# Linear attention and a token layer on one core: the middle key tile projected in row tiles into the banks of h, with a new order

## The chip, the core and the metric

The kernel runs on one core of a Trainium2 chip. The metric is device time in microseconds (us): the median of three timed runs, 710.31 us before the change (709.31 to 710.52). Beside the timed runs one execution was profiled; all rows of a view come from it.

Engines: PE multiplies matrices (PEld is its loading of weights), DVE works on vectors, ACT evaluates functions and copies, POOL (GpSimd) is a second vector engine, SP issues the DMAs. Each runs its own instructions in program order and waits on semaphores for the others.

## The reference

Linear attention over 8 batches, 8 heads, 576 tokens and 64 dimensions with exponential features, then a layer over all 4608 tokens.

```python
def phi(x):
    proj = np.einsum('bhsd,df->bhsf', x, w_phi)
    proj = proj - np.max(np.abs(proj), axis=-1, keepdims=True)
    return np.concatenate([np.exp(proj), np.exp(-proj)], axis=-1)
q_p, k_p = (phi(q), phi(k))
kv = np.einsum('bhsf,bhsd->bhfd', k_p, v)
z = np.sum(k_p, axis=2)
num = np.einsum('bhsf,bhfd->bhsd', q_p, kv)
den = np.einsum('bhsf,bhf->bhs', q_p, z)[..., None] + 1e-06
x = (num / den).transpose(0, 2, 1, 3).reshape(B * S, H * D)

h = x @ w_in
e = np.exp(h - np.max(h, axis=-1, keepdims=True))
solu = h * (e / (np.sum(e, axis=-1, keepdims=True) + 1e-09))
mu, var = np.mean(solu, -1, keepdims=True), np.var(solu, -1, keepdims=True)
out = ((solu - mu) / np.sqrt(var + 1e-06) * g_ln) @ w_out
```

`w_phi` is 64 x 128, `w_in` 512 x 1024, `w_out` 1024 x 512.

## The kernel before

**Attention in 16 units.** A unit u is half a batch: two pairs of heads, each pair two heads of 64 dimensions that fill the 128 partitions. The 576 keys of each pair are four tiles of 128 tokens and a half tile of 64; the half tiles of the unit's two pairs lie together in one *middle key tile* of 128 tokens. So a unit has three key groups (`GROUPS`, line 32): four outer tiles of the first pair (g = 0), the middle tile (g = 1), four outer tiles of the second pair (g = 2).

Keys are projected on PE by `kp`. For the outer groups `k_rows` calls `by_rows` (line 527): for each tile one matmul a head, with the 64 rows of that head alone (128 tokens by 128 features, 64 x 128 of the array), the two heads into two different banks; 8 matmuls in all. For the middle tile `k_mid` calls `by_block` (line 536): one matmul over all 128 rows against `wph`, which holds `w_phi` twice, block-diagonally, with zeros elsewhere; it gives 256 columns in one bank. Behind the projection DVE takes `km` (maximum of absolute values, writes `m`) and `ks` (subtraction, writes `dk`), both reading the bank; ACT takes two exponentials of `dk` into `ek`. All are called `pjk`, `m`, `dk` and `ek` in the profile. [...]

Queries of units 0 to 2 (`Q_PLAIN`) go the same way (`pjq`, `dq`, transposed as `dT`); later ones are projected transposed (`pq`, four half blocks a pair of heads), turned by DVE (`blk`), and get their maximum over a small PE transposition (`mtp`), DVE `mt`, POOL `mb` and a second one (`mcp`). `visit` (line 599) then does on PE, in one piece, the numerators of the pair before (`num`), the products of keys and values (`kvT`) and the denominators (`den`).

**Tokens in 36 tiles of 128.** `moe_h` (line 1084) makes `h` in two halves of 12 matmuls (fp32r, from high and low parts of x and `w_in`); `moe_max` (DVE, `nm`), `moe_exp` (ACT, `eu`) and `moe_u` (DVE, `eu<-h,eu`) read its banks in turn, and the last of them frees them. The result is transposed by a DVE pass (`ub`) and DMAs (`du`, `uTs`), split into high and low parts (`uhs`, `uls`), and multiplied with `w_out` by `moe_o` (`o`, two halves of 12).

**PSUM.** Eight banks: `a` has three buffers of one bank, `kv` one, `h` one buffer of two banks, `mo` two of one (`PSUM_BUFS`, line 46). `h` serves the token tiles. In the units of `EARLY` (0, 1, 2) key and query groups use `h` and `mo`; from unit 3 on, all key groups, `pq`, `mtp`, `mcp`, `num` and `den` share `a`.

**What sets the order.** Each step is an entry of a plan (`op`, `add`) with an engine, what it comes after, and the buffers that it takes and uses. `SEQUENCE` (line 57) is a list of 2623 numbers: the entries in the order in which they are written out, which is the order on every engine and on SP's queue; `Plan.order` (line 240) asserts that nothing stands ahead of what it needs. A buffer goes to whoever comes next in that list. The costs in the entries play no part in the written order.

Of the kernel before, what the change touches and what calls it, by code (L numbers as in the profile page):

```python
# [18 lines left out]
DM, DF = 512, 1024  # L19
NTOK = B * S  # L20
P = 128
# [1303 lines left out]
```

## Time and profile before

| what | us |
|---|---|
| median of three timed runs | 710.31 |
| the profiled execution, whole | 708.93 |
| its span, first to last instruction | 707.1 |
| PE busy | 694.5 |
| POOL busy | 512.3 |
| DVE busy | 478.1 |
| ACT busy | 368.2 |

The busy time of the groups that the change touches, over the whole span: the 512 records of outer key tiles (`pjk`, 64*128) 39.4 us, the 32 records of middle tiles (`pjk`, 128*128) 10.8 us, and the three `h` groups of 288 records 93.7, 89.5 and 89.0 us. Records of PE overlap, so that their lengths add up to more than their share of time; what a piece costs is read from the starts of its neighbours. DVE's idle time ahead of `nm` is 64.5 us in sum, ended by PE's `h`.

### The profile page before, as it was taken

The page shows a single profiled execution, that of the slowest core. Times are in us where ns is not written, and L with a number is a line of the kernel's source. Part 1 is how long each engine was busy: PE and PEld are TensorE (multiplying, and loading weights), DVE is VectorE, ACT ScalarE, POOL GpSimd, SP SyncE. Part 2 cuts the span into 40 slices and gives each one's busy share as a digit, 9 for nine tenths or more (in the row PEclk, how much of TensorE's full clock was granted, in tenths as well). Part 3 has the DMA queues.
Part 4 walks back from the last instruction along what each step waited for, and adds up shares of the span by engine and source line. Part 5 has one row for each costly group of instructions (what it writes and reads, how often), then busy time and mean ns, then how long its engine had stood idle before and what let it go on. Part 6 is the DMA issues. An engine that isn't in the chain of part 4 may idle for free.

```text
span 707.1 us, 13443 instructions
## 1 busy us (share of the span) xinstructions
PE 694.5 (98%) x4894; PEld 520.2 (74%) x4894; DVE 478.1 (68%) x795; ACT 368.2 (52%) x684; POOL 512.3 (72%) x500
## 2 busy tenths in 40 slices
PE   8999999999999999999999999999999999999997
PEld 6666676777777777777777777777787777788886
DVE  6999787647867668577675777857567775354531
ACT  4997744626545564455554656535554554233231
POOL 1156999997878888789788997978868878361341
PEclk9999999999999999999999999999999999999999
DMA  8954465545575565566545555556374435320331
GB/s 293 339 191 120 114 199 163 157 115 161 162 214 151 143 201 151 166 167 193 144 116 162 188 164 156 173 164 191 107 201 156 127 109 149 94 94 24 124 116 67
DMA packets 113778, 110.04 MB, mean 156 GB/s; under 512 B 57648, under 2 KB 91184, under 8 KB 113200
## 3 DMA queue, kind: packets, MB, share of 16 engines
q1 hardware_dynamic: 113712, 109.18, 51.5%
q8 instruction: 39, 0.64, 0.4%
q14 instruction: 27, 0.22, 0.1%
HBM read 76.75 MB, written 32.39 MB: 154 GB/s over the span
## 4 chain that ended last, share of the span: by engine, by line
PE 64%; POOL 1%; DMA 1%; issue 1%; DVE 1%; ACT 0%; SPq 0%; ACTq 0%; POOLq 0%
PE h L271 22%; PE o L271 22%; PE kvT L271 6%; PE num L271 5%; PE pjk L271 3%; PE pq L271 3%; PE den L271 2%; DMA du<-ub 1%; DMA uTs<-du 0%; POOL xa L271 0%; PE uT L271 0%; PE mcp L271 0%; PE mtp L271 0%; POOL uls L271 0%; POOL zacc L271 0%
## 5 line engine op out<-in xcount | busy, mean ns | idle before, releaser
L271 ACT ACTIVATE ek<-dk 128x512 f32<-128x512 f32 (+1 forms) x160 | 87.2, 583 | 64.5 <-DVE dk L271 64.4
L271 PE MATMUL o<-w_out_h,uhs 128*128 128x512 f32 x264 | 105.3, 399 | 0.0
L271 PE MATMUL o<-w_out_h,uls 128*128 128x512 f32 x264 | 103.3, 391 | 0.1
L271 PE MATMUL o<-w_out_l,uhs 128*128 128x512 f32 x264 | 103.1, 390 | 0.0
L271 POOL TENSOR_TENSOR uls<-uTs,uhs 128x1024 fp32r<-128x1024 f32 x33 | 79.1, 2396 | 25.3 <-ACT uhs L271 22.9
L271 PE MATMUL h<-win_h,mxh 128*128 128x512 f32 x288 | 93.7, 406 | 0.0
L271 PE MATMUL h<-win_l,mxh 128*128 128x512 f32 x288 | 89.5, 392 | 0.0
L271 PE MATMUL h<-win_h,mxl 128*128 128x512 f32 x288 | 89.0, 390 | 0.0
L271 DVE TENSOR_REDUCE nm<-h 128x1 f32<-128x1024 f32 x36 | 43.7, 1215 | 64.5 <-PE h L271 64.4
L271 ACT ACTIVATE fq<-pT 128x576 f32<-128x576 f32 x104 | 68.4, 676 | 20.9 <-DVE pT L271 20.8
L271 POOL TENSOR_TENSOR zt<-ek 128x512 f32<-128x512 f32 x52 | 67.2, 1292 | 15.1 <-ACT ek L271 14.2
L271 POOL TENSOR_TENSOR hq<-rawq,hq 64x1152 fp32r<-64x1152 f32 x26 | 68.9, 2652 | 8.9 <-ACT hq L271 4.2
L271 PE MATMUL num<-fq,kvf 128*64 128x288 f32 x512 | 68.9, 412 | 0.8 <-DMA kvf<-dk 0.5
L271 ACT ACTIVATE eu<-h,nm 128x1024 f32<-128x1024 f32 x36 | 40.2, 1116 | 56.4 <-DVE nm L271 45.8
L271 DVE STREAM_TRANSPOSE blk<-pq 128x288 f32<-128x288 f32 x104 | 45.3, 459 | 28.2 <-PE pq L271 23.7
L271 DVE TENSOR_REDUCE m<-pjk 128x4 f32<-128x512 f32 (+1 forms) x80 | 48.5, 622 | 22.9 <-PE pjk L271 22.7
L271 PEld LDWEIGHTS h<-win_h,mxl 128*128 128x128 f32 x288 | 54.0, 188 | 12.1
L271 PEld LDWEIGHTS h<-win_l,mxh 128*128 128x128 f32 x288 | 54.0, 188 | 12.0
L271 PE MATMUL kvT<-ek,rawv 128*64 128x256 f32 x512 | 61.1, 380 | 0.0
L271 POOL TENSOR_TENSOR blk<-blk,mcol 128x1152 f32<-128x1152 f32 x26 | 55.4, 2131 | 5.7 <-PE h L271 3.5
L271 PEld LDWEIGHTS h<-win_h,mxh 128*128 128x128 f32 x288 | 50.7, 189 | 10.7 <-DVE kvs L271 0.5
L271 PEld LDWEIGHTS o<-w_out_h,uls 128*128 128x128 f32 x264 | 49.5, 188 | 11.5 <-POOL uls L271 0.7
(109 smaller groups left out, 1425.4 us busy)
## 6 DMA issues: line engine op xcount, KB each, us to landing
du<-ub SPq DMA_DIRECT2D x33, 512.0 KB, 2.9
uTs<-du SPq DMA_DIRECT2D x132, 128.0 KB, 3.1
rawq<-in_q SPq DMA_DIRECT2D x26, 576.0 KB, 4.6
rb<-d SPq DMA_DIRECT2D x64, 144.0 KB, 3.3
out<-os SPq DMA_DIRECT2D x35, 256.0 KB, 2.9
rawk<-in_k SPq DMA_DIRECT2D x32, 256.0 KB, 4.5
rawv<-in_v SPq DMA_DIRECT2D x32, 256.0 KB, 3.8
dk<-kvs SPq DMA_DIRECT2D x28, 192.0 KB, 1.9
```

Of the source, the lines that this page charges most:

```text
L271: return self.tc.keep_in_program_order(method(*args, **kwargs))
```

## The change

From unit 3 on the middle tile is projected by a new `k_mid_rows`: two matmuls, each head with its own 64 rows and its own 128 columns of `wph`, the first into the first bank of `h`, the second into the second. `tokens`, which gives DVE its view of a projection, reads such a tile as two pieces of 128 columns, 512 apart. The entry `kp` of the middle tile takes `h` in place of a buffer of `a`. Units 0 to 2 keep `by_block`.

```diff
+    def k_mid_rows(st):
+        pj = bank("h", [P, DF], "pjk")
+        for j, r in enumerate(HEADS):
+            nc.tensor.matmul(
+                pj[:, 512 * j : 512 * j + F], lhsT=st["rk", 1][r, :P], rhs=wph[r, j * F : (j + 1) * F],
+                start=True, stop=True,
+            )
+        st["pj", 1] = {None: pj}
...
     def tokens(pj, n):
+        if pj.shape[1] == DF:
+            return pj.rearrange("p (j c) -> p j c", j=2)[:, :, :F]
         return pj[:, : n * F].rearrange("p (t f) -> p t f", f=F)
...
             ktag = K_BANKS[g] if u in EARLY else "a"
-            add(("kp", g), "tensor", mm32(256) if g == 1 else 4 * 224, z, k_mid if g == 1 else k_rows,
-                (ktag,) if g == 1 else (g, ktag), [("kl", g), ("abs", "wp")],
-                banks(ktag, "pj", g), [("rk", g)])
+            if g == 1 and u not in EARLY:
+                ktag = "h"
+                add(("kp", g), "tensor", 224, z, k_mid_rows, (), [("kl", g), ("abs", "wp")], banks(ktag, "pj", g), [("rk", g)])
+            else:
...
 SEQUENCE = (
-    99, 3, 2, 88, 0, 132, 126, 7, 136, 102, 4, 100, 101, 90, 103, 104, 5, 127, 107, 95, 89, 91, 230, 130, 14,
...
```

`SEQUENCE` is new as a whole; all engines' instructions stand in another order. Three places of it follow.

**Unit 3, PE.** Before, from the end of token tile 0 (`h`, low part of x) to the start of token tile 2:

```order
L271 MATMUL h<-win_h,mxl 128x512 x2
L271 MATMUL dT<-ident,dq 128x128 x3
L271 MATMUL pjk<-wph,rawk 128x256
L271 MATMUL mtp<-ident,m_1218 36x128
L271 MATMUL dT<-ident,dq 128x128 x3
L271 MATMUL pjk<-wph,rawk 128x128 x8
L271 MATMUL pq<-hq,w_hh 128x288
L271 MATMUL pq<-hq,w_l_76 128x288
L271 MATMUL h<-win_h,mxh 128x512 x2
```

After, the same stretch:

```order
L271 MATMUL h<-win_h,mxl 128x512 x2
L271 MATMUL mtp<-ident,m_1256 36x128
L271 MATMUL dT<-ident,dq 128x128 x6
L271 MATMUL pjk<-wph,rawk 128x128 x10
L271 MATMUL mcp<-ident,mb_77 128x128
L271 MATMUL pq<-hq,w_hh 128x288
L271 MATMUL pq<-hq,w_l_76 128x288
L271 MATMUL h<-win_h,mxh 128x512 x2
```

The middle tile (128x256) stood between transpositions; its two matmuls now stand directly behind the 8 of the second outer group, as one row of 10, with the small transposition `mcp` behind them.

**Unit 3, DVE.** Before, the passes from the maximum of token tile 0 on:

```order
L271 TENSOR_REDUCE nm<-h 128x1
L271 TENSOR_REDUCE m<-pjk 128x2
L271 TENSOR_REDUCE mt<-mtp 36x32
L271 TENSOR_TENSOR dk<-pjk,m 128x256
L271 TENSOR_TENSOR eu<-h,eu 128x1024
L271 TENSOR_REDUCE m<-pjk 128x4 x2
```

After:

```order
L271 TENSOR_REDUCE nm<-h 128x1
L271 TENSOR_REDUCE mt<-mtp 36x32
L271 TENSOR_TENSOR eu<-h,eu 128x1024
L271 TENSOR_REDUCE m<-pjk 128x2
L271 TENSOR_TENSOR dk<-pjk,m 128x256
L271 TENSOR_REDUCE m<-pjk 128x4 x2
```

The two passes over the middle tile (`m` 128x2 and `dk` 128x256) stood ahead of the pass that frees `h` (`eu<-h,eu`) and now stand behind it.

**Unit 5, PE.** Before, from the end of token tile 4 on; the rows of `o` behind begin half an `o`, 12 matmuls:

```order
L271 MATMUL h<-win_h,mxl 128x512 x2
L271 MATMUL pjk<-wph,rawk 128x128 x8
L271 MATMUL pjk<-wph,rawk 128x256
L271 MATMUL o<-w_out_h,uhs 128x512
L271 MATMUL o<-w_out_l,uhs 128x512
L271 MATMUL o<-w_out_h,uls 128x512
```

After, from the end of token tile 4 to the first rows of half an `o`:

```order
L271 MATMUL h<-win_h,mxl 128x512 x2
L271 MATMUL pjk<-wph,rawk 128x128 x8
L271 MATMUL mcp<-ident,mb_77 128x128
L271 MATMUL o<-w_out_h,uhs 128x512
L271 MATMUL o<-w_out_l,uhs 128x512
L271 MATMUL o<-w_out_h,uls 128x512
```

And from the last row of the same half `o` to the next token tile:

```order
L271 MATMUL o<-w_out_h,uls 128x512
L271 MATMUL pjk<-wph,rawk 128x128 x2
L271 MATMUL pq<-hq,w_hh 128x288
L271 MATMUL pq<-hq,w_l_76 128x288
L271 MATMUL pq<-hq,w_hh 128x288
L271 MATMUL pq<-hq,w_l_76 128x288
L271 MATMUL pq<-hq,w_hh 128x288
L271 MATMUL pq<-hq,w_l_76 128x288
L271 MATMUL h<-win_h,mxh 128x512 x2
```

The two matmuls of the middle tile stand alone now, between half an `o` and the projections `pq`, ahead of the next token tile's `h`; before, the block-diagonal one stood directly behind the outer group.

**The start, SP.** Before, the first loads:

```order
L271 DMA rawk<-in_k 128x128
L271 DMA wph<-in_w_phi 128x256
L271 DMA rawk<-in_k 128x512
L271 DMA rawq_165<-in_q 128x128
L271 DMA rawq_167<-in_q 128x512
L271 DMA wraw_169<-in_w_in 128x2048
L271 DMA rawq_171<-in_q 128x512
```

After:

```order
L271 DMA rawk<-in_k 128x512
L271 DMA rawk<-in_k 128x128
L271 DMA wph<-in_w_phi 128x256
L271 DMA rawq_165<-in_q 128x512
L271 DMA rawq_167<-in_q 128x512
L271 DMA rawq_169<-in_q 128x128
L271 DMA vz_72<-in_v 64x128
L271 DMA rawv<-in_v 128x512
L271 DMA rawk<-in_k 128x512
L271 DMA wraw_205<-in_w_in 128x2048
```

`rawk` 128x512 is the first outer key group, 128x128 the middle tile; `rawq` are the query groups, `wraw` a 1 MB piece of `w_in`. The outer keys are ahead of the middle tile now, and all three query groups ahead of `wraw`.

More of the change, by code (lines that the diff above doesn't have):

```diff
@@ L906, in linear_attention_then_moe @@
             ktag = K_BANKS[g] if u in EARLY else "a"
-            add(("kp", g), "tensor", mm32(256) if g == 1 else 4 * 224, z, k_mid if g == 1 else k_rows,
-                (ktag,) if g == 1 else (g, ktag), [("kl", g), ("abs", "wp")],
-                banks(ktag, "pj", g), [("rk", g)])
+            if g == 1 and u not in EARLY:
+                ktag = "h"
+                add(("kp", g), "tensor", 224, z, k_mid_rows, (), [("kl", g), ("abs", "wp")], banks(ktag, "pj", g), [("rk", g)])
+            else:
+                add(("kp", g), "tensor", mm32(256) if g == 1 else 4 * 224, z, k_mid if g == 1 else k_rows,
+                    (ktag,) if g == 1 else (g, ktag), [("kl", g), ("abs", "wp")],
+                    banks(ktag, "pj", g), [("rk", g)])
             for j in heads_of(g):
```

273 rows, old and new, of the table SEQUENCE are left out of this document.

## The prediction

> **What bounds the kernel now.** I read the page's busy shares first, then busy time by stretch, then the waits.
>
> ```profile
> span 707.1 us, 13443 instructions
> PE 694.5 (98%) x4894; PEld 520.2 (74%) x4894; DVE 478.1 (68%) x795; ACT 368.2 (52%) x684; POOL 512.3 (72%) x500
> PE 64%; POOL 1%; DMA 1%; issue 1%; DVE 1%; ACT 0%; SPq 0%; ACTq 0%; POOLq 0%
> 15.00:88.00 73.00, 70.36 (x801) 47.69 (x797) 67.47 (x102) 62.35 (x133) 40.20 (x21) 1.00 0.61 198
> 88.00:580.00 492.00, 489.66 (x3368) 363.38 (x3367) 346.29 (x599) 258.52 (x471) 417.26 (x392) 1.00 0.56 161
> PE pq L271 <- DVE dk L271: 0.5, 1, 0.5
> ```
>
> PE is busy 98% of the span and carries the chain that ended last. Between 88 and 580 us (columns: stretch, length, then busy PE, PEld, DVE, ACT, POOL, clock) it idles 2.34 of 492 us, at full clock. So PE's own work sets the time; waits elsewhere matter where they make PE wait. The last row, of the waits, is the longest wait of PE after 88 us on DVE: a projection `pq` whose bank of `a` DVE had not yet emptied.
>
> Everything below is summed against the profiled execution (708.93 us with what lies around the span) and carried as a difference to the median of the three runs, 710.31 us.
>
> **Cost of the middle tile now.** The timeline around unit 9's tile, alone between two pieces of `h`:
>
> ```profile
> 318.97 0.62 PE L271 MATMUL h<-win_h,mxl 128*128 128x512 f32 x2
> 319.42 0.59 PE L271 MATMUL pjk<-wph,rawk 128*128 128x256 f32 x2
> 319.67 0.82 PE L271 MATMUL h<-win_h,mxh 128*128 128x512 f32 x2
> 320.32 0.62 PE L271 MATMUL h<-win_l,mxh 128*128 128x512 f32 x2
> 320.78 0.39 PE L271 MATMUL h<-win_h,mxl 128*128 128x512 f32 x1
> ```
>
> (Columns: start, length, engine, what.) Starts count, since lengths overlap. A pair of `h` takes 320.78 − 320.32 = 0.46. From 318.97 to 320.32 lie two pairs and the tile: 1.35 − 0.92 = **0.43 us** for the tile.
>
> **Cost of row tiles.** The trace has them for the outer key tiles, 8 matmuls (16 records, two a matmul) a group:
>
> ```profile
> 161.40 0.61 PE L271 MATMUL h<-win_h,mxl 128*128 128x512 f32 x2
> 161.95 1.79 PE L271 MATMUL pjk<-wph,rawk 64*128 64x128 f32 x18
> ...
> 315.45 1.16 PE L271 MATMUL pjk<-wph,rawk 64*128 64x128 f32 x16
> 316.55 0.73 PE L271 MATMUL h<-win_h,mxh 128*128 128x512 f32 x2
> 317.12 0.63 PE L271 MATMUL h<-win_l,mxh 128*128 128x512 f32 x2
> ...
> 66.54 1.16 PE L271 MATMUL pjq<-wph,rawq 64*128 64x128 f32 x16
> 67.53 1.06 PE L271 MATMUL pjk<-wph,rawk 64*128 64x128 f32 x16
> 68.53 0.55 PE L271 MATMUL dT<-ident,dq 128*128 128x128 f32 x3
> ```
>
> A lone group takes 1.10 (315.45 to 316.55); two groups in a row take 1.99, so 16 more records cost 0.89, or 0.056 each. Four records, the new tile, are **0.22** where they stand next to such a group. A group on its own pays for the switch of shape besides: 0.09 ahead (the `h` pair at 161.40 takes 0.55 instead of 0.46), 1.10 − 16 × 0.056 = 0.20 inside, 0.11 behind (the pair at 316.55 takes 0.57). So a lone new tile costs 0.22 + 0.09 + 0.20 + 0.11 = **0.62**, more than the 0.43 it replaces.
>
> In the new order the tile of units 3, 4, 6, 7, 8, 12, 13 and 14 stands directly beside a group of outer tiles; that of units 5, 9, 10, 11 and 15 stands alone. Sum on PE: 8 × (0.22 − 0.43) + 5 × (0.62 − 0.43) = −1.68 + 0.95 = **−0.7 us**. Bounds: −2.7 if lone tiles paid no switch, 0 if the neighbours' switches grew too. I take −0.7, whose parts all have a row.
>
> The Trainium skill, TensorEngine Tiling (Array Packing), section Tiling Modes, says that changing the tiling mode drains TensorE; the trace agrees, with the 0.09, 0.20 and 0.11 above. By that page's doubled rate alone, without the drain, the term would be the −2.7.
>
> **The wait it adds: bank h.** `h` has one buffer of two banks. The new tile may start only when `moe_u` of the token tile before has read it, and the next token tile only when DVE has taken maximum and subtraction of the new tile. The chain of one token tile, undisturbed:
>
> ```profile
> 414.90 0.62 PE L271 MATMUL h<-win_h,mxl 128*128 128x512 f32 x2
> 415.39 0.38 PE L271 MATMUL pq<-hq,w_hh 128*128 128x288 f32 x1
> 415.56 1.22 DVE L271 TENSOR_REDUCE nm<-h 128x1 f32<-128x1024 f32 x1 [1.13 <-PE h L271]
> 416.82 1.12 ACT L271 ACTIVATE eu<-h,nm 128x1024 f32<-128x1024 f32 x1 [0.43 <-DVE nm L271]
> 418.06 1.22 DVE L271 TENSOR_TENSOR eu<-h,eu 128x1024 f32<-128x1024 f32 x1
> 419.34 0.73 PE L271 MATMUL h<-win_h,mxh 128*128 128x512 f32 x2
> ```
>
> PE is free of `h` at 415.39 and may use the bank again at 419.34: **3.95 us**. For the second wait:
>
> ```profile
> L271 DVE TENSOR_REDUCE m<-pjk 128x2 f32<-128x256 f32 x16 | 6.5, 404 | 4.9 <-PE pjk L271 4.9
> L271 DVE TENSOR_TENSOR dk<-pjk,m 128x256 f32<-128x256 f32 x16 | 6.4, 401 | 0.2
> ```
>
> 0.40 + 0.40, and I add 0.5 from the tile's start to DVE's (an estimate from the chain's 0.17 between PE's end and `nm`, on top of the tile's own 0.22 to 0.4): **1.3 us** from tile to next `h`. What is queued behind the waiting matmul is all of PE. Counting PE's work between in the new order against 3.95 and 1.3, at nearly all 13 places there is 3.9 to 14 us ahead and 1.5 to 16 us behind. It falls short here:
>
> Unit 3. Today the chain of token tile 0 is waited out once:
>
> ```profile
> 84.54 0.49 PE L271 MATMUL dT<-ident,dq 128*128 128x128 f32 x3
> 87.23 1.23 DVE L271 TENSOR_TENSOR eu<-h,eu 128x1024 f32<-128x1024 f32 x1 [0.42 <-ACT eu L271]
> 88.52 0.74 PE L271 MATMUL h<-win_h,mxh 128*128 128x512 f32 x2
> ```
>
> `h` follows 3.98 after PE was free (84.54), with one middle tile, one outer group, transposes and `pq` between. In the new order the tile itself waits for `eu` to end at 3.92, and `h` follows 1.3 behind it, with nearly the same work between: +1.3 us.
>
> Unit 5 stands after one outer group, a small transpose and half an `o` (1.1 + 0.1 + 2.8 = 4.0). Today's DVE at that place:
>
> ```profile
> 162.06 1.23 DVE L271 TENSOR_REDUCE nm<-h 128x1 f32<-128x1024 f32 x1 [1.66 <-PE h L271]
> 163.20 0.68 DVE L271 TENSOR_REDUCE m<-pjk 128x4 f32<-128x512 f32 x1
> ...
> 165.12 1.22 DVE L271 TENSOR_TENSOR eu<-h,eu 128x1024 f32<-128x1024 f32 x1
> ```
>
> Three passes of 0.68 stand between `nm` and `eu` then and later, so the bank is free at 166.34, 4.4 after 161.95; PE arrives at 4.0: 0.4. Behind the tile come 1.3 us of PE work and on DVE one more 0.68 pass ahead of the tile's two: 0.2 more. Together +0.6.
>
> Units 9 and 10 have 3.8 to 3.9 us of work ahead: +0.2 for both. Sum of these waits: **+2.1 us**. Bounds: +0.5 (if PE comes late there anyway, half of unit 3's remains) to +5 (a DVE that is 0.4 late at each of seven places with under 4.5 us behind). I take the row sums.
>
> **What the new order moves at the start.**
>
> ```profile
> 9.59 0.67 PE L271 MATMUL pjq<-wph,rawq 128*128 128x256 f32 x2 [1.67 <-issue]
> 11.27 1.16 PE L271 MATMUL pjq<-wph,rawq 64*128 64x128 f32 x16 [0.67 <-DMA rawq<-in_q]
> 9.41 1.28 DVE L271 TENSOR_TENSOR dk<-pjk,m 128x512 f32<-128x512 f32 x2
> ```
>
> The group at 11.27 waits 0.67 for its queries, whose load stands behind the 1 MB `w_in` piece on SP; in the new order it stands ahead of it. What is late next is its bank (`h`, in the early units), which DVE's `dk` passes leave at 10.69; so PE gains 11.27 − 10.69 = 0.58: **−0.6 us**. The 1.67 stays: DVE sets it, with the same passes. Bounds: 0, since DVE is 67.47 of 73 us busy from 15 to 88 us and may hold PE up again there; −1.3, with one weight pass of 0.68 that DVE now makes later.
>
> **Bank a.** The middle tile no longer takes one of three banks of `a`. The wait of 0.5 quoted first is of that kind: −0.5, bounds 0 and −2.3 (all the idle time from 88 to 580 us). All other moves (other neighbours, other moments of loads and evictions, over two thousand entries) I cost at nothing: the same engines do the same work, and the cover is the PE queue that leaves 2.34 us idle; if it goes, each new wait of PE costs its length, 0.3 to 0.7 by the waits shown. The wider DVE read (two banks instead of one) I cost at nothing as well, since the 128x4 passes are set by their elements, 0.68 for 512.
>
> Sum: −0.7 + 2.1 − 0.6 − 0.5 = +0.3. Forecast **710.6 us**: no change that a measurement can tell (0.2%, 1.4 us, is about what this kernel's runs can distinguish).
>
> **Rivals.**
>
> *Faster.* The bank's waits are mostly covered: at unit 3 PE may come late for its own reasons (today a transpose and a group wait in just that stretch), which halves +1.3, and units 5, 9, 10 keep 0.4; `a` gives twice 0.5. −0.7 − 0.6 − 1.0 + 1.0 = −1.3, and with lone tiles that pay half a switch and the start's far bound −2.5: about 707.8. For it: the separations at ten of thirteen places are wide. Against: 3.95 us is a chain of three passes, which nothing shortens.
>
> *Slower.* Bank h becomes the wait of many units, not two. In units 4, 6, 7, 8 and 13 PE has 3.7 to 4.6 us between tile and next `h`, and DVE has statistics, transposes or maxima of 2 to 4 us queued ahead of the tile's subtraction. It decides once DVE is about 0.5 us behind there: then each loses some 0.6, 5 × 0.6 = 3.0, on top of the forecast: 713.6. For it: every pass in these queues is 0.4 to 1.3 us. Against: DVE idles 146 of 492 us.
>
> *It doesn't do what it says.* If the two row tiles did not run side by side, each tile costs 0.22 more, 13 × 0.22 = +2.9: 713.5. Against: 0.056 a record is what pairs in two banks already reach, and the new tile writes two banks.
>
> **How the numbers follow.** Forecast 0.37, faster 0.35, slower by the bank 0.25, not side by side 0.03. The forecast's own range is 708.9 to 711.7; drawn out to where the rivals' bulk lies, 706.8 to 713.8 leaves out 2 in 10. Faster 0.35, same 0.37, slower 0.28.
>
> **What would show it.** Groups of 20 records `pjk` and lone ones of 4; the first 0.22 longer than today's, the second about 0.6 of PE. `h` after unit 3's tile some 5.3 us after PE left token tile 0. The third query group without a wait for its load near 10.7 us. Waits of `h` or `pjk` on DVE `dk` or `eu` in units other than 3, 5, 9 and 10 would make the slower rival right; PE idle from 88 to 580 us under 2.3 us, the faster one. It is wrong altogether if the reordered rest moves PE's waits by more than 3 us.

## The result, and the profile after

The changed kernel takes **722.35 us** (median of 4 runs, 720.41 to 723.59) where the kernel before takes 710.41 beside it: ratio 1.0158, interval 1.0131 to 1.0186. Forecast was 710.6, with a range up to 713.8; the time lies 8.6 us above that range. The profiled execution of the changed kernel, the slowest of its four runs, takes 723.59 us, 14.7 more than that of before (708.93), which is faster than all its timed runs. Ratios leave out four slow executions, one each of e2, e9 and e12 below and one of the kernel before; the profiled one of e9, at a granted clock of 0.75, is among them and isn't read.

The page after, its lines for the span, busy time, granted clock of PE (40 slices) and the chain that ended last:

```profile
span 721.8 us, 13497 instructions
PE 702.0 (97%) x4920; PEld 525.1 (73%) x4920; DVE 483.1 (67%) x795; ACT 369.6 (51%) x684; POOL 512.0 (71%) x500
PEclk8998989999999999999999999999999999999999
PE 78%; DVE 8%; DMA 6%; issue 2%; SPq 2%; ACT 2%; POOL 2%; DVEq 0%; POOLq 0%; ACTq 0%
```

PE is busy 7.5 us longer although its work should have shrunk, three of the first six slices of the clock show an 8, and DVE holds 8% of the chain, where it held 1%. Busy time by stretch, cut where the granted clock changes (columns: stretch, length, busy PE, PEld, DVE, ACT, POOL, then clock, DMA share, GB/s):

```profile
10.88:17.71 6.83, 6.35 (x42) 5.21 (x41) 4.91 (x10) 4.82 (x10) 0.00 (x0) 0.50 0.97 342
17.71:51.84 34.13, 32.84 (x400) 21.32 (x399) 34.10 (x46) 29.77 (x62) 9.00 (x5) 1.00 0.79 287
51.84:58.67 6.83, 5.10 (x30) 3.93 (x32) 6.80 (x9) 5.01 (x12) 3.93 (x2) 0.50 0.32 89
...
96.22:103.04 6.82, 6.38 (x18) 4.90 (x19) 3.72 (x8) 5.07 (x10) 6.53 (x8) 0.50 0.03 8
```

Three stretches of 6.83 us ran at half clock, all in the first 104 us: 3 × 6.83 × 0.5 = up to 10.2 us of PE's work lost. In the profiled execution of before the clock is 1.00 from 15 us to the end. Later, the same stretch in both kernels, before first:

```profile
104.00:590.00 486.00, 483.69 (x3314) 360.23 (x3313) 340.51 (x592) 257.80 (x469) 407.29 (x388) 1.00 0.55 159
...
104.00:590.00 486.00, 481.25 (x3315) 357.33 (x3315) 340.00 (x588) 252.03 (x458) 404.19 (x377) 1.00 0.55 161
```

PE idles 486 − 483.69 = 2.3 us before and 4.75 after. By the starts of `kvT` of corresponding pairs, 11.8 of the 14.7 us are lost by 104 us and about 3 more by 590 us. The longest waits of PE after (columns: who waits for whom, us in all, times, longest):

```profile
PE pjk L271 <- ACT E L271: 2.1, 3, 1.1
PE pjk L271 <- DMA wph<-in_w_phi: 1.8, 1, 1.8
PE dT L271 <- DVE dq L271: 1.8, 1, 1.8
PE pjq L271 <- DVE dk L271: 1.7, 2, 1.3
...
PE pjk L271 <- DVE eu L271: 1.4, 2, 1.2
```

The longest of before, 1.7 us of `pjq` on its own issue, is in both. Of those shown only the last, 1.4 us, is the wait for bank `h` that the prediction priced. `h` waiting for `dk` is not among them.

### The profile page after: what moved, and what is told of

It is laid out like the page before. It is cut to its first block, busy times and chain, and to the rows that moved or that the text cites. A ratio compares the mean times of both kernels' runs of the same rounds, so it can differ in the third digit from the quotient of the medians.

```text
span 721.8 us, 13497 instructions
## 1 busy us (share of the span) xinstructions
PE 702.0 (97%) x4920; PEld 525.1 (73%) x4920; DVE 483.1 (67%) x795; ACT 369.6 (51%) x684; POOL 512.0 (71%) x500
## 4 chain that ended last, share of the span: by engine, by line
PE 78%; DVE 8%; DMA 6%; issue 2%; SPq 2%; ACT 2%; POOL 2%; DVEq 0%; POOLq 0%; ACTq 0%
PE h L271 25%; PE o L271 25%; PE kvT L271 8%; PE num L271 7%; PE pjk L271 5%; PE pq L271 4%; PE den L271 3%; DVE w L271 3%; SPq L271 2%; DVE m L271 2%; DMA uTs<-du 1%; DMA out<-os 1%; DVE dk L271 1%; DMA rawq<-in_q 1%; DMA du<-ub 1%
## 5 line engine op out<-in xcount | busy, mean ns | idle before, releaser
L271 DVE TENSOR_REDUCE nm<-h 128x1 f32<-128x1024 f32 x36 | 43.8, 1216 | 61.2 <-PE h L271 61.0
L271 DVE TENSOR_TENSOR eu<-h,eu 128x1024 f32<-128x1024 f32 x36 | 43.9, 1221 | 34.0 <-ACT eu L271 33.8
L271 PEld LDWEIGHTS o<-w_out_h,uhs 128*128 128x128 f32 x264 | 49.8, 188 | 10.8 <-issue 0.5
```

What stands on the lines that cost most here:

```text
L271: return self.tc.keep_in_program_order(method(*args, **kwargs))
```

## The experiments

OLD and NEW stand for the two lists `SEQUENCE` of before and after; `X + rest of Y` means the entries X, then all others in the order of Y. "Row tiles" are middle tiles as two row tiles in bank `h`. The kernel before ran beside each group of experiments; its medians there were 710.7 to 711.6 us, its single runs 706.7 to 715.5. Ratios are against these. Where a run splices the two lists, row tiles are in those units alone whose middle tile comes from NEW.

| run | edit | median us | ratio (interval) |
|---|---|---|---|
| e11_after_again | the changed kernel | 721.03 | 1.012 (1.0088 to 1.0152) |
| e1_warm | five more warm-up matmuls | 720.23 | 1.0126 (1.0074 to 1.0178) |
| e2_wph_first | `w_phi` loaded first | 722.22 | 1.0112 (1.0035 to 1.019) |
| e5_unit3 | unit 3's row tile earlier | 726.23 | 1.0211 (1.016 to 1.0263) |
| e6_block_in_h | block-diagonal, in `h` | 726.02 | 1.0227 (1.0164 to 1.0291) |
| e3_early_before | OLD up to 274, then NEW | 717.25 | 1.0096 (1.0061 to 1.013) |
| e7_early_unit3 | e3 and e5 together | 721.43 | 1.0154 (1.0091 to 1.0217) |
| e9_start_after | NEW up to 490, then OLD | 717.46 | 1.0078 (1.005 to 1.0107) |
| e10_rest_after | OLD up to 490, then NEW | 714.67 | 1.0057 (1.0033 to 1.008) |
| e14_late_half | OLD up to 1545, then NEW | 716.6 | 1.0085 (1.0058 to 1.0112) |
| e4_early_after | NEW up to 243, then OLD | 716.4 | 1.0072 (1.0045 to 1.01) |
| e16_first70_new | NEW up to 70, then OLD | 711.73 | 1.0009 (0.9991 to 1.0027) |
| e17_70_to_243_new | NEW only from 70 to 243 | 716.25 | 1.0085 (1.0057 to 1.0112) |
| e18_dq_first | e17, one DVE pass earlier | 713.96 | 1.004 (1.0018 to 1.0061) |
| e8b_rows_alone | OLD, row tiles in 8 units | 716.83 | 1.0074 (1.0047 to 1.0102) |
| e15_five_rows | OLD, row tiles in 5 units | 711.43 | 1.0026 (1.0003 to 1.0048) |
| e12_loads_new | OLD, SP's queue of e4 | 758.71 | 1.0657 (1.0616 to 1.0698) |
| e13_loads_old | e4, SP's queue of OLD | 752.88 | 1.0603 (1.0571 to 1.0634) |

**Is it the row tiles or the order?** First theory: the order brings waits, and these bring half clock. Rival: row tiles and their bank cost at all 13 places.

e6 takes the row tiles away and leaves the bank and the order:

```diff
-        for j, r in enumerate(HEADS):
-            nc.tensor.matmul(
-                pj[:, 512 * j : 512 * j + F], lhsT=st["rk", 1][r, :P], rhs=wph[r, j * F : (j + 1) * F],
-                start=True, stop=True,
-            )
+        nc.tensor.matmul(pj[:, : 2 * F], lhsT=st["rk", 1][:, :P], rhs=wph, start=True, stop=True)
...
     def tokens(pj, n):
-        if pj.shape[1] == DF:
-            return pj.rearrange("p (j c) -> p j c", j=2)[:, :, :F]
```

> The changed kernel with the middle tiles of units 3 to 15 block-diagonal again (one matmul of 256 columns), but still into bank h and in the new order; DVE reads one bank. Order theory: the shape of the matmul is worth the 0.7 us that the sum gave it, so 722 to 724. Rival (the row tiles themselves, or DVE's reads across two banks, cost the time): most of the 11.9 us comes back, 711 to 715.

Nothing came back (726.02, 2 us above what the order theory gave), so neither the shape of the matmuls nor DVE's reads of two banks is the cost. e4 has no row tile at all, only the start of the new order, and e3 the reverse:

```diff
-SEQUENCE = OLD
+SEQUENCE = NEW[:243] + rest of OLD
```

> The kernel before with the first 243 entries in the new order (until about 53 us), the rest as before; no row tile in it at all. Theory of the clock and of the early waits: 6 to 8 us more than before, 716.5 to 718.5, with two stretches at half clock. Bank h: 710.4, as before.

```diff
-SEQUENCE = NEW
+SEQUENCE = OLD[:274] + rest of NEW
```

> The changed kernel with the first 274 entries of the order as they were before (until about 58 us), the rest in the new order; all row tiles stay. Theory of the clock and of the early waits: the fourth and fifth visit come about 7 us earlier again; the wait and the half-clock stretch at unit 3 stay: 714 to 716. Bank h: no change, 721 to 723.

The start alone costs 0.72%, as expected. e3 stays 1.25 us above the 714 to 716 expected of it, less than its interval is wide; it hints that more than the start is at work. A cut at entry 490 (about 104 us; the two lists share all but six entries there) gives the two halves, with e11 on the same chip:

```diff
+SEQUENCE = NEW[:490] + rest of OLD
...
+SEQUENCE = OLD[:490] + rest of NEW
```

> The new order up to its entry 490 (unit 3's keys, unit 3's row tile in bank h, about 104 us), the order of before from there, block-diagonal middle tiles in a from unit 4 on. Theory: the first 104 us carry 11.8 of the change's 14.7 us in the profiled executions, by waits and stretches of half clock: 8 to 10 us slower than before, ratio 1.011 to 1.014, with two or three stretches of half clock before 104 us. Rival (the 12 later row tiles and the order behind them carry most): 1 to 3 us slower, the wait of unit 3 and the start, 1.001 to 1.004.

> The other half: the order of before up to its entry 490, with unit 3 block-diagonal in a, and the new order from there, with the 12 row tiles of units 4 to 15 in bank h. Theory: what the profiled executions show from 104 us on, 3 us slower than before, ratio 1.003 to 1.005, with no stretch of half clock that before has not; by the rows 7 adjacent tiles and 5 lone ones give -0.5 of it, the rest is waits of PE in the new order. Rival: 8 to 10 us slower, 1.011 to 1.014.

> The changed kernel as it is, for a ratio on the same chip as the two halves: 1.013 to 1.019, and the excesses of the two halves add up to its own within 2 us.

The first half costs 0.78%, the second 0.57%; their sum, 1.35%, is the whole within its interval (1.2%). So the split adds up, but neither half lies in the range of the theory: the start is cheaper (0.78%, expected 1.1 to 1.4) and the rest dearer (expected 0.3 to 0.5) than the profiled executions had it, and the second half holds its 12 row tiles beside the order. Behind 104 us e10's trace has the same picture as the changed kernel:

```profile
104.00:590.00 486.00, 480.69 (x3326) 355.79 (x3315) 335.96 (x585) 254.04 (x461) 404.97 (x378) 1.00 0.55 159
...
262.95 1.16 PE L264 MATMUL pjk<-wph,rawk 64*128 64x128 f32 x14 [0.99 <-ACT E L264]
```

PE idles 5.3 us instead of 2.3, and its longest single wait is an outer key group in bank `a` that ACT's eviction `E` has not yet emptied. That is e10's own wait; where the changed kernel has its longest one, the timeline shows what ACT was busy with:

```profile
570.20 1.15 PE L271 MATMUL den<-fq,kvf 128*32 128x288 f32 x16
570.40 1.10 ACT L271 ACTIVATE eu<-h,nm 128x1024 f32<-128x1024 f32 x1
571.49 0.61 ACT L271 CAST mxh<-xa 128x512 fp32r<-128x512 f32 x1
572.00 0.70 ACT L271 COPY E<-num 128x288 f32<-128x288 f32 x2
572.46 0.37 PE L271 MATMUL pjk<-wph,rawk 64*128 64x128 f32 x1 [1.11 <-ACT E L271]
```

The key group stands directly behind `num` and `den` and takes their banks next; ACT comes to them behind a token tile's `eu` and a cast. e14 was to place these losses:

> The order of before up to its entry 1545 (about 375 us), the new order with row tiles in bank h for units 11 to 15 from there. If the 4 us that the run e10_rest_after lost lie evenly over the new order's waits (bank a on ACT's evictions at 404, 480 and 572 us: 0.7, 0.3 and 1.1 us): 2 us slower than before, ratio 1.002 to 1.004. If they lie in units 4 to 10: 1.000.

Its edit is `OLD[:1545] + rest of NEW`. It cost 0.85%, more than the whole rest, so it tells little: 3.8 of its us are lost at the seam itself, where PE waits 2.07 us for an eviction `os`, a wait that the traces of neither whole list have there, and where a stretch of half clock follows.

**Where in the start?** The cut at entry 70 (about 15 us):

```diff
+SEQUENCE = NEW[:70] + rest of OLD
...
+SEQUENCE = OLD[:70] + those of NEW[:243] not yet placed + rest of OLD
```

> The kernel before with only its first 70 entries in the new order (loads, keys and queries of unit 0, to about 15 us), the rest as before; no row tile. In the traces of the changed kernel DVE's first maximum starts at 6.2 to 6.5 us instead of 4.9, since PE waits 1.1 to 1.8 us for w_phi, which is loaded third; DVE is busy nearly throughout from 15 to 64 us, so it cannot win that back. If this late start is the new start's cost: with a stretch of half clock 1.5 to 3 us slower, ratio 1.002 to 1.004; if it is all of it, 5 us, 1.007. If nothing of it: 1.000.

> The complement: the first 70 entries as before, the entries up to 243 in the new order, the rest as before; no row tile. Theory: the new order of units 0 to 2 between 15 and 46 us (dT waiting 1.8 us on DVE dq near 50 us, and the stretch of half clock behind it) carries the larger part: 2 to 4 us slower, ratio 1.003 to 1.006. Rival (the late start carries it all): 1.000.

The first 15 us cost nothing that can be measured (1.0009), although PE waits 1.3 us for `w_phi` there. Entries 70 to 243, units 0 to 2 between 15 and 50 us, carry all of it, 1.0085. One group of DVE passes stands out there. The group, the two last of the three steps that turn each weight block into `w`, in e17 and then in e16 (columns: line, engine, what, count, busy us, mean ns, idle ahead):

```profile
L263 DVE SCALAR_TENSOR_TENSOR w<-wraw,w 128x1024 uint32<-128x1024 uint32 x16 | 21.9, 1389 | 0.0
...
L263 DVE SCALAR_TENSOR_TENSOR w<-wraw,w 128x1024 uint32<-128x1024 uint32 x16 | 19.2, 1217 | 0.0
```

The mean is 1382 to 1392 ns in all eight traces that have the new order there (the changed kernel, e1, e2, e4, e5, e6, e11, e17). Where the old order stands, it is 1216 to 1229 in six (before, e3, e7, e8b, e14, e16), but 1345 and 1347 in e10 and e15. The timelines show which passes, before first (POOL's rows and these of DVE alone):

```profile
44.38 3.48 POOL L271 TENSOR_TENSOR wsum<-w,w 128x1024 f32<-128x1024 f32 x1
44.43 1.21 DVE L271 SCALAR_TENSOR_TENSOR w<-wraw,w 128x1024 uint32<-128x1024 uint32 x1
47.96 1.21 DVE L271 SCALAR_TENSOR_TENSOR w<-wraw,w 128x1024 uint32<-128x1024 uint32 x1
48.62 5.25 POOL L271 TENSOR_TENSOR wsum<-wsum,w 128x1024 f32<-128x1024 f32 x2 [0.76 <-ACT w L271]
...
48.93 2.81 POOL L271 TENSOR_TENSOR wsum<-w,w 128x1024 f32<-128x1024 f32 x1
50.04 2.78 DVE L271 SCALAR_TENSOR_TENSOR w<-wraw,w 128x1024 uint32<-128x1024 uint32 x1
51.81 3.22 POOL L271 TENSOR_TENSOR wsum<-wsum,w 128x1024 f32<-128x1024 f32 x1
52.74 0.68 DVE L271 TENSOR_TENSOR dq<-pjq,m 128x512 f32<-128x512 f32 x1
53.57 1.51 PE L271 MATMUL dT<-ident,dq 128*128 128x128 f32 x6 [1.76 <-DVE dq L271]
53.94 2.17 DVE L271 SCALAR_TENSOR_TENSOR w<-wraw,w 128x1024 uint32<-128x1024 uint32 x1
```

Before, a weight pass of DVE that meets POOL's sums `wsum` takes 1.21 and POOL pays: the two sums from 48.62 on, behind DVE's pass of 47.96 to 49.17, take 5.25, of which 4.70 lie behind that pass. The row at 44.38 warns against reading too finely: POOL's sum is recorded 0.05 ahead of DVE's pass there, and still POOL pays, 3.48 in place of some 2.35. After, POOL is first by 1.11, and DVE pays: its pass starts at 50.04, POOL's sum ends at 48.93 + 2.81 = 51.74, and DVE's ends 1.08 behind that, at 52.82. The second is alike: POOL's ends at 55.03, DVE's at 56.11. Behind the first slow pass stands `dq`, and behind `dq` PE's `dT` waits 1.76. The Trainium skill, SBUF — State Buffer, sections SBUF: two separate sides and Who interferes with whom, says that a DVE instruction with two inputs in SBUF and a GpSimd instruction that reads SBUF shut each other out for a whole instruction, and that issue order decides who waits; the trace agrees, with the 1.08 left over each time. That the passes' operands all lie in SBUF is read from the kernel.

The old order can fall the same way. e10 and e15 have it in this stretch entry for entry (e15 up to entry 1018, behind 200 us), and there the first of the two passes is held up; e15:

```profile
45.49 2.36 POOL L264 TENSOR_TENSOR wsum<-w,w 128x1024 f32<-128x1024 f32 x1
45.68 3.25 DVE L264 SCALAR_TENSOR_TENSOR w<-wraw,w 128x1024 uint32<-128x1024 uint32 x1
48.85 0.68 DVE L264 TENSOR_TENSOR dk<-pjk,m 128x512 f32<-128x512 f32 x1
49.59 1.16 PE L264 MATMUL pjq<-wph,rawq 64*128 64x128 f32 x14 [1.99 <-DVE dk L264]
```

POOL's sum starts 0.19 us ahead of the pass and ends at 47.85, the pass 1.08 behind that. `dk` comes late, PE waits 1.99 for it, and 3.41 us at half clock follow (51.31 to 54.72): 1.99 + 1.7 = 3.7. By the starts of `kvT`, held against before's, e15 loses 3.8 us between 33 and 50 us, and e10, with the same picture, 3.5. The other traces with the old order there, whose passes took 1.21 to 1.24, lose nothing in that stretch. So one and the same order has both outcomes, and a held-up pass with what follows it is shown to cost some 3.5 us. What the new order does is to put POOL's sum first in every trace of it that was read. It also bears on the spread of single runs: the profiled executions of e10 and e15 lie 2.6 and 3.3 us above their medians.

e18 moves the awaited pass ahead of the slow one:

```diff
 e17, DVE
+    (1, 'qs', 2, 0)
     ('wb', 7, 1)
...
-    (1, 'qs', 2, 0)
```

> The run e17_70_to_243_new with one DVE pass moved: unit 1's dq (the one for which dT waits 1.8 to 1.9 us near 52 us) ahead of the weight pass that took 2.9 us instead of 1.2 beside POOL's wsum. If PE's wait there is the cost: the wait goes, and 2 to 3.5 us of e17's 6 with it, ratio 1.003 to 1.006. Rival (DVE is full from 15 to 64 us, so what it does first only moves the wait): another wait of PE on DVE of 1 to 2 us appears behind it, and the ratio stays at 1.007 to 1.009.

The ratio falls from 1.0085 to 1.004, as the first reading wanted (the intervals still overlap slightly), and the wait of `dT` is gone. But its profiled execution, the slowest of its twelve runs, shows the rival's wait too:

```profile
47.98 2.34 POOL L263 TENSOR_TENSOR wsum<-w,w 128x1024 f32<-128x1024 f32 x1 [2.65 <-PE den L263]
48.13 2.74 DVE L263 TENSOR_SCALAR w<-wraw 128x1024 uint32<-128x1024 uint32 x1
50.79 0.68 DVE L263 TENSOR_TENSOR dk<-pjk,m 128x512 f32<-128x512 f32 x1
51.52 1.16 PE L263 MATMUL pjq<-wph,rawq 64*128 64x128 f32 x14 [3.27 <-DVE dk L263]
```

Here another weight pass, with one input, met the sum 0.15 us behind its start, took 2.74 us (0.69 on average before), and held `dk` and PE. So e18 moved the hold-up more than it removed it, and doesn't settle the cause by itself. The order is shown to be the cost by the cuts, and the price of a held-up pass by e10 and e15; that such passes make up the whole 6 us of e17 is not shown.

Two runs aimed at the same question gave no answer. e12 and e13 exchanged SP's queue alone between OLD and e4:

> The kernel before, all engines in its old order, with only SP's queue in the order that the start has in the run e4_early_after (outer keys of unit 0 first, w_phi third, all three query groups ahead of the 1 MB piece of w_in). No row tile. If the loads are what the new start costs: about 5 us slower than before, ratio 1.006 to 1.009. If the order on the computing engines is: within 1.5 us, 0.998 to 1.002; a wait of PE for w_phi of 1 to 2 us near 5 us may show by both.

> The other half: the computing engines in the order of the run e4_early_after (243 entries in the new order, then the old one), SP's queue as before. No row tile. If the computing engines' order is what the start costs: 4 to 6 us slower, ratio 1.005 to 1.008, with the wait of dT on DVE dq of 1.8 us near 50 us and a stretch of half clock behind it. If the loads are: within 1.5 us of before.

Both lost 42 to 48 us, in steps spread over the whole program, most of them far behind the entries that were exchanged. Presumably the buffers that DVE and SP share were handed out in another order too. They say nothing about the start.

**Half clock.** e1 lengthens the warm-up, e2 loads `w_phi` first:

```diff
-NWARM = 6
+NWARM = 11
```

> The changed kernel with 11 instead of 6 matmuls of zeros at the start, so that PE is not idle while it waits 1.83 us for the load of wph; nothing else is changed and no wait is shortened. Theory of the clock (the time was lost because waits of PE in the first 104 us brought three stretches of 6.83 us at half the granted clock): the stretch from 10.88 to 17.71 us goes or shrinks, and the time falls by 2 to 3.5 us, to 719 to 720.5. Theory of the waits alone: 722.3, no change within 0.5. Theory of bank h (the middle tiles' waits on the bank of h cost the time): 722.3.

> The changed kernel with the load of wph moved from third to first on SP. Theory of the clock: the wait of 1.83 us goes and with it the first half-clock stretch: 4 to 5 us less, 717.5 to 718.5. Waits alone: 1.2 to 1.8 less, 720.5 to 721. Bank h: no change, 722.3.

e1's trace has no half clock before 50 us any more, and its time is as expected, but e11 shows that the changed kernel alone gives such times too (721.03), and its trace has no half clock before 50 us either: no verdict. e2 missed: 722.22, with single runs from 714.41 to 725.59. Across all runs the loss by clock, (1 − mean granted clock) × span, is on average 8.8 us for the four runs of the changed kernel, 5.0 for e11, 5.9 for e17, and 1.8 to 3.1 for before and e16. So half clock is a part of the loss, up to 2 to 6 us more than the kernel before has, and it varies from run to run. The profiled execution of before, at 1.00 to its end, is not typical of that kernel.

**Unit 3.** e5 puts the row tile, its maximum and its subtraction ahead of token tile 0, e7 does the same on top of e3:

```diff
 NEW, unit 3
+    (3, 'kp', 1)  (3, 'km', 1)  (3, 'ks', 1)
     ('moe', 0, 'h', 0)
...
-    (3, 'kp', 1)  (3, 'km', 1)  (3, 'ks', 1)
```

> The changed kernel with one thing moved: unit 3's middle tile, its maximum and its subtraction stand ahead of token tile 0's h instead of behind the second outer key group, so that the tile has bank h before token tile 0 takes it and waits for nothing. Order-and-clock theory (waits of the early order bring stretches of half clock): PE's wait of 1.2 to 1.4 us on DVE eu at 95 us goes, and with it the third stretch of half clock (96.2 to 103.0 us); 717.5 to 720. Rival (the time lies in the row tiles and in bank h at all 13 places, one of which is eased here): only the wait goes, about 1.3 us: 721, and the stretch stays. The first two stretches stay by both.

> The changed kernel with its first 274 entries in the order of before, and unit 3's middle tile moved ahead of token tile 0 as in the run e5_unit3. Order-and-clock theory: of the stretches of half clock at most the first stays; 711.5 to 714.5. Rival (row tiles and bank h at all 13 places): the order of the start gives what it gave alone (717.3) and the tile of unit 3 about 1.3 more: 716.

Both missed, and neither theory had it: the wait moved and doubled.

```profile
86.78 1.49 DVE L263 TENSOR_TENSOR w<-w,cms 128x512 f32<-128x512 f32 x1
...
88.64 0.42 DVE L263 TENSOR_TENSOR dk<-pjk,m 128x256 f32<-128x256 f32 x1
89.22 1.19 PE L263 MATMUL h<-win_h,mxh 128*128 128x512 f32 x2 [2.46 <-DVE dk L263]
```

Now token tile 0 waits 2.46 us until DVE, behind its weight passes, comes to the tile's two.

**Row tiles in the old order.** e8b places row tiles in OLD wherever bank `h` is free, next to an outer group; e15 leaves out the three units where e8b waited:

```diff
+ROWS = (4, 6, 7, 8, 9, 10, 11, 15)
...
-            if g == 1 and u not in EARLY:
+            if g == 1 and u in ROWS:
```

> The order of before throughout, with row tiles in bank h for units 4, 6, 7, 8, 9, 10, 11 and 15 alone, each directly beside the first outer key group of its unit, ahead of the next token tile's h, with its DVE maximum and subtraction done before that h; the other units stay block-diagonal in a. Theory (row tiles are cheap, the order of the first 104 us is what costs): 8 times 0.21 us less on PE, some of it given back in waits of h on DVE: 0 to 1.7 us below before, ratio 0.9976 to 1.000. Rival (row tiles in bank h cost the time, 11.9 us for 13 of them): 8 of 13, about 7 us slower than before, ratio 1.010. A third, weaker: each next h waits for DVE about 0.5 us, 2 to 3 us slower, 1.003 to 1.004.

> As the run e8b_rows_alone, but row tiles only in units 6, 7, 9, 10 and 15; units 4, 8 and 11, where that run waited (h on DVE dk 0.7 and 0.9 us, mcp on POOL mb 2.0 us and num on DVE 1.1 us behind unit 8's tile), stay block-diagonal in a. Theory (a row tile costs only where it displaces DVE's passes): 0 to 1 us below before, ratio 0.998 to 1.001. Rival (each row tile in bank h costs by itself): five eighths of that run's 5.3 us, 3.3 us slower, 1.0046.

e8b is 0.74% slower, against the theory. Its `kvT` starts, held against before's, lose 3.3 us at one place, unit 8:

```profile
284.11 0.69 DVE L264 TENSOR_TENSOR dk<-pjk,m 128x512 f32<-128x512 f32 x1 [1.03 <-DMA dk<-kvs]
285.06 0.28 POOL L264 COPY mb<-mt 36x128 f32<-36x128 f32 x1 [3.76 <-DVE mt L264]
285.39 0.33 PE L264 MATMUL mcp<-ident,mb 128*128 128x128 f32 x1 [1.95 <-POOL mb L264]
```

The tile's `dk` had taken its buffer earlier than in OLD, so DVE waited 1.03 us for another one, everything behind it came late, and PE waited 1.95 for `mcp`. At units 4 and 11 `h` waited 0.73 and 0.92 us for the tile's `dk`. e15, without these three, is at 1.0026: between theory and rival, with an interval that reaches to both. So what a row tile in bank `h` costs by itself stays open within 0 to 0.5% for five of them; that their gain of 0.2 us each, 1 us in all, doesn't come through is what both runs show.

No kernel here beats the one before.

## Why the prediction was wrong, point by point

**The step that failed** is the sentence "All other moves (other neighbours, other moments of loads and evictions, over two thousand entries) I cost at nothing". Its reasons were that the same engines do the same work and that PE's queue covers the rest, at 2.34 us idle. Neither holds: which of DVE and POOL is held up depends on who is first (1.21 or 2.78 us for the same pass), PE waits behind DVE, and half clock comes on top, so that a new wait costs more than its length. The runs put +0.85% on the order of entries 70 to 243 alone (e17) and +0.57% on what is new behind 490 (e10, order and 12 row tiles together), about 6 and 4 us. The second part is explained less well: PE idles 3 us more there in e10's trace, in many short waits, and no run took them apart. The closing remark, that the forecast is wrong altogether if the reordered rest moves PE's waits by more than 3 us, is what happened: up to 104 us the listed waits of PE sum to 5.9 us before and 11.1 after. It was given no chance of its own.

**Full clock.** The sum took the clock of the profiled execution of before, 1.00, for granted, and had no term for losing it. The waits that the new order has in the first 104 us go with half clock: up to some 6 us more of loss than the kernel before has, in the first four runs, and 2 to 3 in e11 and e17.

**Cost of row tiles on PE: right.** The changed kernel's group and tile of unit 7, and a lone tile near 390 us (two records a matmul):

```profile
249.90 1.39 PE L271 MATMUL pjk<-wph,rawk 64*128 64x128 f32 x20
251.22 0.50 PE L271 MATMUL o<-w_out_h,uhs 128*128 128x512 f32 x1
...
390.47 0.49 PE L271 MATMUL pjk<-wph,rawk 64*128 64x128 f32 x4
390.89 0.50 PE L271 MATMUL o<-w_out_h,uhs 128*128 128x512 f32 x1
391.23 0.40 PE L271 MATMUL o<-w_out_l,uhs 128*128 128x512 f32 x1
```

A group with its tile takes 251.22 − 249.90 = 1.32, the forecast 1.10 + 0.22. The lone tile takes 0.42 to the next row, and that row 0.11 more than the 0.23 of its kind: 0.53 (391.23 − 390.89 = 0.34). It is 0.62 with the 0.09 ahead, which these rows don't show. That the tiles would not run side by side is refuted, and e6, which undoes them, gained nothing. That the −0.7 comes through in the time is not shown; e8b and e15 speak against it.

**Bank h: right in kind, unit 3's price too small.** Unit 3:

```profile
92.41 0.27 PE L271 MATMUL mtp<-ident,m 128*36 128x128 f32 x1
...
95.10 1.23 DVE L271 TENSOR_TENSOR eu<-h,eu 128x1024 f32<-128x1024 f32 x1 [1.08 <-ACT eu L271]
96.38 0.80 PE L271 MATMUL pjk<-wph,rawk 64*128 64x128 f32 x4 [1.15 <-DVE eu L271]
...
98.51 1.06 PE L271 MATMUL h<-win_h,mxh 128*128 128x512 f32 x2
```

PE was free of `h` at 92.41, the tile came at 96.38, 3.97 later (forecast 3.92), and `h` 6.1 later (forecast 5.3; the last 2.3 of the 6.1 ran at half clock). Unit 5 waited 0.23 at 177.97 instead of 0.4, and the rival by which many units wait for the bank did not come. It did in e8b, where the tiles were placed without care for DVE. What unit 3's wait costs is more than the +1.3 of the sum, since half clock follows it: in e3's trace, with the old order up to 58 us, `kvT` falls 4.8 us behind between 69 and 97 us, with a wait of 1.2 and 6.83 us at half clock. By the medians it is less: e3 and e10, which differ in entries 274 to 490 alone, are 0.4% apart, with intervals that overlap.

**The start.** The load wait of the third query group is gone as forecast, and DVE's wait has its place:

```profile
5.80 1.76 PE L271 MATMUL pjk<-wph,rawk 128*128 128x256 f32 x18 [1.83 <-DMA wph<-in_w_phi]
11.48 2.08 PE L271 MATMUL pjq<-wph,rawq 64*128 64x128 f32 x16 [0.48 <-DVE dk L271]
```

But `w_phi`, moved to third place on SP, now comes 1.83 us late, which the prediction did not look at, though it printed the order. In place of −0.6 us e16 measures +0.09% ± 0.18%, no change.

**Bank a: wrong in sign.** One tenant fewer was to save 0.5 us. That wait, of `pq` on DVE's `dk`, is gone. But behind 104 us PE now waits for `a` on ACT's `E` 2.1 us in all, and not at all before, since the new order puts key groups directly behind the products whose banks they need.

**The faster rival's far sum.** By its own terms it comes to −3.0 instead of −2.5: five half switches of 0.20 and 0.7 more at the start, on top of −1.3. Nothing else rests on it.

## What to carry to other kernels

A new order as a whole is a change of its own, and a larger one than the edit that asked for it: price it by the engines that feed the bound one, pass by pass, at the places where they are full, or give it a chance of its own in the forecast. Where DVE and POOL passes that both read SBUF meet, look at which is first, since the other pays the whole overlap; let the one with slack pay. And before a large reordering is judged, cut it: the old list up to an entry and the new one behind it, where both lists have placed nearly the same entries, tells in a few runs which part costs. One profiled execution shows one outcome of such a race: where two engines start within a few tenths of a us of each other, look at traces of several runs.

## What the hardware showed that was not expected

The same DVE pass took 1.21 us or 2.78, up to 3.25, and a shorter one 0.69 or 2.74, by whether POOL's sum was first. In these traces a recorded lead of POOL of 0.15 us and more held DVE up; one of 0.05 did not.

Half clock came in stretches of 3.41, 6.83 or 10.24 us, in the changed kernel near waits of only 0.5 to 1.8 us. The stretch from 51.84 on began 0.03 us into the wait of 1.76 for `dq`, so it wasn't that wait that brought it; PE had waited 1.26 for `dk` up to 50.17. Cut into windows of 3.41 us along the stretches' own edges, the trace has PE busy 1.75 us in the window up to 10.88, 2.12 in that up to 51.84 and 1.96 in that up to 96.22. Each stretch went on behind windows with 1.68 to 2.97 and ended behind one with 3.41. Cut alike, 16 traces (all but those of before, e9, e12 and e13) have PE busy less than 2.2 us in the window ahead of every stretch. The reverse doesn't hold: 1.82 us in e17, from 50.46 on, brought none. In e14 one stretch starts near 388.2, behind a wait of 2.07, and one near 439.4, behind 1.35.

The Trainium skill, TensorE: Matmul & The Clock Gate, Part 1, has a free-running activity window of about 3.4 us, which fits the lengths and the variation from run to run; its advice, in the section Why this matters for your kernels, to avoid gaps of over some 3 us, would have let all these waits pass, and here the trace decides. That little work in a window brings the stretch is read from the traces; it wasn't tested by itself.
